# Cosine attention followed by a token-mixing MLP: a hand-written order of instructions changed in ten places

## The chip, the cores and the metric

The kernel runs on one core of one Trainium2 chip. The metric is device time in microseconds (us) of one execution; lower is better. The engines are named as in the profile: PE (TensorE matmul) and PEld (its weight loads), DVE (VectorE), ACT (ScalarE), POOL (GpSimd), and SP (SyncE), which here issues every DMA.

## The reference

Two operations follow each other. With B = 8 batches, 8 heads, S = 576 positions and head size 64, in float32:

```python
r = np.maximum(x, 0.0)                                  # for q and k
phi = np.concatenate([r * cos_w, r * sin_w], axis=-1)   # 64 -> 128 features
kv  = np.einsum('bhsf,bhsd->bhfd', k_p, v)
z   = np.sum(k_p, axis=2)
num = np.einsum('bhsf,bhfd->bhsd', q_p, kv)
den = np.einsum('bhsf,bhf->bhs', q_p, z)[..., None] + 1e-06
x   = num / den                                         # back to (B, S, 512)

wq, wk = x @ w_q, x @ w_k                               # 512 -> 64
W_tok  = scale * np.einsum('bsd,btd->bst', wq, wk)
mixed  = np.einsum('bst,btd->bsd', W_tok, x)
out    = np.maximum(mixed, 0.0) @ w_out                 # 512 x 512
```

The kernel takes the second part as wq @ (wk^T x), so that no 576 x 576 matrix is made.

## The kernel before

The work is cut into 16 **halves** H (half the heads of a batch; H = 2b + h) for the attention, 8 **batches** b for the mixing, and 36 **row tiles** of 128 rows for the product with w_out. Each piece of work is a small function, a *step*. One long string, ORDER, lists the steps; the kernel walks it once and issues each step's instructions on its engine. An engine runs its instructions in the order in which they were issued and waits where an operand or a buffer isn't ready, so ORDER sets the order on each engine. A word such as `QT10:2` or `EP22@A` is a step, its number, after a colon the PSUM bank from which it writes (eight banks, most results take a pair), and after @ the engine (A = ACT, V = DVE, G = POOL). A trailing a or b is one half of a step whose work is split in two.

The steps of a half H:

- LK, LQ, LV: loads of k, q, v (two DMAs each, 288 KB); five buffers of each, used in turn.
- RK, RQ: relu to bf16 (lines 203, 205). CV, VS: v to bf16 (209, 211), then multiplied by the cos and sin table on DVE (line 234); VG does both in one on POOL (line 248).
- QT: q transposed on PE (line 295 "wide", 9 transposes of 128x128; line 301 "narrow", 18 of 64 rows). The tuple QT_WIDE says which halves are wide. QM multiplies that by the table on DVE: two instructions for a wide half (line 316), one for a narrow one (line 320).
- KV: the kv matrix on PE (lines 275, 285); KE takes it out of PSUM (lines 209, 213).
- N(2H), N(2H+1): numerator and denominator on PE (line 340; some have two short matmuls more, line 348, that add epsilon). EP adds epsilon to the denominator (357 on ACT, 359 on DVE), RC and RJ are reciprocals (378, 381), X multiplies (line 393), all into the token matrix x of the batch.

The steps of a batch b: XT or XR transpose x on PE (406, 419), XE takes that out into xT (209, 213); WK and WQ are the products with w_k and w_q on PE (439, 452), KW and QW take them out; KX is wk^T x on PE (466), XK takes it out, XA and XB copy it to the other partitions; MX is the mixing product on PE (489, four a batch: MX(4b) to MX(4b+3)), ME its relu (500 on ACT, 502 on DVE).

WO is a row tile's product with w_out on PE (line 509, four matmuls of 128x512), OE takes it out into one of 16 output buffers (the number behind its colon), ST stores it (line 519, 256 KB). WO needs only mixed batches, so WO steps stand between other steps all the way to the end.

PSUM banks, output buffers and the pairs of buffers of most tiles are written again while the kernel runs; a step that writes one waits for the step that read it last. So the bank number in a word decides for whom the step waits.

Of the kernel before, what the change touches and what calls it, by code (L numbers as in the profile page):

```python
# [37 lines left out]
EP8@V EP9@V RJ4 RQ6a@A XT5:0 X8 XB1@G XE5@A X9 KV7:2 RQ6b@G QM7 VG6b MX6:4 KE7@A XT4:0 ME6@A MX7:2
XE4@V QT6:6 ME7@A N15:4 QM6 RK6a@A MX3:2 N14:0 CV6a@G LV11a EP15@A RK6b@A WK2:6 ME3@A VS6a WQ2:7
KW2@A RC14 KV6:2 RC15 QW2@A X14 CV8a@G KX2:7 KE6@A CW4@G X15 CW2@A N13:2 CW3@A CW5@V N12:0 EP13@V  # L40
XR7:4 XK2@V WO8:6 RC13 XA2@A X13 EP12@A CV8b@G XE7@A WO2:7 RC12 VS8 WO7:2 CV9b@A RQ8a@G LQ13a LQ11b
LQ10a LK11b LK11a LQ11a LV11b X12 OE8:0@A MX8:4 WO6:3 RQ8b@A RK8a@G ME8@V OE7:1@A XR6:0 RQ9a@G WO1:6
CV9a@A XE6@V RQ9b@G OE2:2@A QT8:4 VS9 OE6:3@A RK8b@A QT9:0 RK9a@G OE1:4@A WK3:3 QM9 WO4:2 RK9b@G
KW3@A OE4:5@A ST4 LV12a LK10a LQ10b LV10a LV10b LQ12a KV8:0 QM8 XB2@A KV9:6 KE8@A MX9:4 KE9@A MX11:0
VG11a N16:2 ME9@A ME11@V WQ3:6 RC16 KX3:7 X16 QW3@A MX10:0 XK3@A N17:4 ME10@A N19:2 RK11@V N18:6
EP19@A WO11:0 EP17@V RQ11@A RC17 EP18@V X17 WO5:1 VG11b OE11:6@V ST11 LK12a LK10b LQ13b LV12b LK12b
LQ12b QT11:4 OE5:5@A RC19 RC18 X18 WO9:0 X19 WO10:1 OE9:7@A RQ10@G KV11:2 XA3@A QM11 XR8:6 KE11@A
XR9:4 VG10a LV15a LV13a LQ14b LV14b LQ14a LV13b XE8@A QT10:2 XE9@V WO0:5 QM10 OE10:8@A MX13:0
OE0:6@A MX12:6 N22:2 WO12:4 RQ13a@G ME12@V EP22@A XB3@A ME13@A RC22 VG10b WK4:5 X22 MX14:0 KW4@A
N23:6 ME14@V MX15:2 EP23@A KX4:5 RK10@A WQ4:0 XK4@V RQ13b@G RC23 WO3:1 ME15@A X23 XA4@G XB4@A QW4@A  # L50
RQ12b@G KV10:2 OE3:9@V RQ12a@A QT13:6 OE12:10@A ST12 LK13b LK13a LV14a VG12 MX18:0 WO14:5 QM13
# [3 lines left out]
EP24@V RK13@A RJ12 QT14:0 X24 WO21:2 KW5@A X25 CV14a@G KV13:4 OE21:10@A ST21 LQ15b LQ15a ST3 LK15a
QM14 CV14b@A WQ5:3 KE13@A KX5:2 VS14 XR12:4 XK5@A N27:0 XE12@A N26:6 RK14a@G WO20:2 RC26 EP27@V RC27
XA5@G RK14b@A X27 WO19:4 XB5@G QW5@A VG15b X26 KV14:0 OE19:2@A MX21:6 KE14@A MX23:4 WO18:3 ME21@V
ME23@A OE20:10@V ST20 ST17 ST8 ST9 XR13:4 RQ15a@G MX22:6 RQ15b@V MX20:0 ME22@A WO15:2 VG15a XE13@V
ME20@A N28:6 OE18:9@V OE15:14@A N29:0 EP28@A QT15:4 RK15@A EP29@V RC28 WK6:3 RC29 X29 WO25:2 KW6@A
QM15 OE25:15@A ST25 ST7 ST15 ST18 ST0 ST10 ST16 ST5 ST14 ST6 KV15:0 X28 KX6:3 KE15@A WQ6:2 N31:0  # L60
XR14:6 EP31@V QW6@A N30:4 XE14@V WO23:2 EP30@A XK6@A RJ15 X30 XA6@G WO24:3 OE23:7@A ST23 ST1 XB6@G
X31 WO26:2 OE24:0@A ST24 ST19 XR15:0 MX25:4 MX27:6 XE15@V ME25@A WO22:3 ME27@V WK7:0 OE26:9@V ST26
MX24:6 KW7@A MX26:4 WQ7:1 ME24@A ME26@V KX7:0 OE22:8@V ST22 WO28:2 XK7@A QW7@V XA7@G WO27:3
# [7 lines left out]
def kernel(  # L71
# [240 lines left out]
    def QM(H, ps, eng):  # L312
        if H in QT_WIDE:
            q_t = qt_wide(place["QT", H]).rearrange("p c (r d) -> p r c d", r=2)
            for r in range(2):
                V.tensor_mul(  # L316
                    qm_b[H % NQM][:, :, r, 0:C, :],
                    q_t[:, r].unsqueeze(1).to_broadcast([P, 2, C, H2]), qtab)
# [280 lines left out]
```

## Time and profile before

| what | value |
|---|---|
| time, median of 3 runs | 119.17 us (118.6 to 119.84) |
| the profiled execution: its own time / its span | 118.42 / 116.6 us |
| PE busy | 94.7 us (81% of the span) |
| DVE, ACT, POOL busy | 90.5, 83.1, 64.8 us |
| DMA | 39.38 MB, mean 338 GB/s |
| granted TensorE clock | 1.000 |

The span runs from the first to the last instruction; the execution's own time is 1.8 us longer. In the timelines that follow, each row is a run of equal instructions: start in us from the beginning of the span, time from the first start to the last end, engine, line, operation, output <- inputs, and the count; in brackets the engine's idle time ahead of it and what ended that. Rows of PE overlap a little, since matmuls are pipelined: the next row's start tells where the row's work has left the engine.

### The profile page before, as it was taken

Reading aid. Unit: us, or ns where it says so; the run is one execution under the profiler, and the core shown is the slowest. Engines: PE = TensorE matmul, PEld = TensorE weight load, DVE = VectorE, ACT = ScalarE, POOL = GpSimd, SP = SyncE. Lnnn points to the kernel's source line nnn. Section 1 sums busy time; section 2 is a strip of 40 time slices with the busy share of each in tenths; the row PEclk is TensorE's granted clock in tenths of the full one; section 3 lists DMA queues with packets and bytes.
Section 4 is the critical chain, followed back from the end, with each engine's and each line's share of the span. In section 5 each row is a group of like instructions: output and inputs, shape, how many; then the busy total and the mean of one; then the engine's idle time right before and its main releaser. Section 6 shows DMA issues by size and latency. Waiting matters only on the chain.

```text
span 116.6 us, 4971 instructions
## 1 busy us (share of the span) xinstructions
PE 94.7 (81%) x2104; PEld 65.1 (56%) x2118; DVE 90.5 (78%) x162; ACT 83.1 (71%) x147; POOL 64.8 (56%) x65
## 2 busy tenths in 40 slices
PE   0005967779796797999999899999999999999970
PEld 0004856657576776647775656656775576463420
DVE  2008999799798999889799887898997996795620
ACT  4547558499899987898884878986888774546340
POOL 7600399861634796477298498899659901002000
PEclk9999999999999999999999999999999999999999
DMA  3999999999999999999979999987898467999874
GB/s 90 349 386 399 401 372 346 388 389 396 386 392 384 387 387 387 391 390 384 383 251 302 351 397 371 358 266 258 270 340 293 169 236 271 403 367 400 337 306 173
DMA packets 20662, 39.38 MB, mean 338 GB/s; under 512 B 3232, under 2 KB 3232, under 8 KB 20640
## 3 DMA queue, kind: packets, MB, share of 16 engines
q1 hardware_dynamic: 20640, 39.07, 92.4%
q8 instruction: 16, 0.26, 0.9%
q14 instruction: 6, 0.05, 0.1%
HBM read 29.62 MB, written 9.44 MB: 335 GB/s over the span
## 4 chain that ended last, share of the span: by engine, by line
PE 48%; DMA 26%; DVE 14%; SPq 4%; issue 3%; ACT 1%; DVEq 0%; ACTq 0%
PE ps L509 24%; DMA qraw<-in_q_dram 16%; DMA vraw<-in_v_dram 5%; DMA kraw<-in_k_dram 5%; PE ps L340 5%; DVE qm L316 5%; SPq L145 4%; PE ps L285 3%; PE ps L489 3%; PE ps L419 3%; PE ps L439 3%; DVE xT L213 3%; PE ps L466 3%; PE ps L452 2%; DVE x L393 2%
## 5 line engine op out<-in xcount | busy, mean ns | idle before, releaser
L248 POOL TENSOR_TENSOR v<-vraw,vtab 128x1152 bf16<-128x1152 f32 (+1 forms) x12 | 35.5, 2969 | 6.5 <-DVE qm L316 2.2
L509 PE MATMUL ps<-wow,mix 128*128 128x512 bf16 x130 | 33.3, 380 | 1.2 <-issue 0.3
L393 DVE TENSOR_TENSOR x<-ps,rec 128x640 bf16<-128x640 f32 x32 | 25.4, 818 | 0.7
L209 ACT COPY o<-ps 128x512 f32<-128x512 f32 x25 | 14.5, 592 | 9.2 <-PE ps L509 8.1
L509 PEld LDWEIGHTS <-mix 128*128 128x128 bf16 x144 | 12.5, 98 | 14.4 <-issue 1.7
L295 PE MATMUL ps<-ident,rq 128*128 128x128 bf16 x117 | 9.5, 233 | 12.0 <-ACT rq L203 11.0
L316 DVE TENSOR_TENSOR qm<-ps,qtab 128x1152 bf16<-128x1152 bf16 x26 | 18.3, 749 | 0.8 <-PE ps L295 0.7
L234 DVE TENSOR_TENSOR v<-vb,vtab 128x2304 bf16<-128x2304 bf16 (+1 forms) x11 | 11.8, 1084 | 7.7 <-ACT vb L209 7.3
L500 ACT ACTIVATE mix<-ps 128x576 bf16<-128x576 f32 x23 | 14.5, 651 | 3.5 <-PE ps L489 2.5
L340 PE MATMUL ps<-kvs,qm 64*128 64x65 bf16 x640 | 14.0, 193 | 2.1 <-ACT kvs L209 1.3
L295 PEld LDWEIGHTS <-rq 128*128 128x128 bf16 x117 | 7.6, 104 | 13.6 <-issue 10.5
L340 PEld LDWEIGHTS <-qm 64*128 64x128 bf16 x640 | 12.6, 96 | 4.2 <-issue 2.3
L203 ACT ACTIVATE rk<-kraw 128x1152 bf16<-128x1152 f32 (+1 forms) x14 | 14.0, 996 | 0.7 <-DMA kraw<-in_k_dram 0.7
L205 POOL TENSOR_SCALAR rq<-qraw 128x576 bf16<-128x576 f32 (+1 forms) x13 | 10.1, 776 | 4.4 <-DMA qraw<-in_q_dram 3.5
L211 POOL TENSOR_SCALAR vb<-vraw 128x576 bf16<-128x576 f32 (+1 forms) x7 | 5.7, 810 | 11.9 <-DMA vraw<-in_v_dram 8.8
L211 POOL TENSOR_SCALAR kx<-kx 64x256 bf16<-64x256 bf16 x9 | 4.1, 457 | 12.6 <-ACT kx L209 11.0
L502 DVE TENSOR_SCALAR mix<-ps 128x576 bf16<-128x576 f32 x9 | 6.8, 757 | 4.0 <-PE ps L489 3.8
L285 PE MATMUL ps<-v,rk 64*64 64x130 bf16 x432 | 9.1, 231 | 0.8 <-POOL v L248 0.7
L209 ACT CAST kvs<-ps 128x260 bf16<-128x260 f32 (+1 forms) x15 | 6.5, 436 | 4.6 <-PE ps L285 3.9
L285 PEld LDWEIGHTS <-rk 64*64 64x64 bf16 x432 | 7.5, 114 | 3.9 <-issue 1.2
L203 ACT ACTIVATE rq<-qraw 128x576 bf16<-128x576 f32 (+1 forms) x10 | 8.3, 832 | 1.1 <-DMA qraw<-in_q_dram 1.1
L213 DVE COPY xT<-ps 128x1280 bf16<-128x1280 bf16 (+1 forms) x9 | 7.3, 813 | 2.2 <-PE ps L419 2.0
(65 smaller groups left out, 137.3 us busy)
## 6 DMA issues: line engine op xcount, KB each, us to landing
kraw<-in_k_dram SPq DMA_DIRECT2D x32, 288.0 KB, 5.9
qraw<-in_q_dram SPq DMA_DIRECT2D x32, 288.0 KB, 5.9
vraw<-in_v_dram SPq DMA_DIRECT2D x32, 288.0 KB, 5.8
out_dram<-o SPq DMA_DIRECT2D x36, 256.0 KB, 3.4
wof<-in_moe_w_out_dram SPq DMA_DIRECT2D x4, 256.0 KB, 5.8
wkf<-in_moe_w_k_dram SPq DMA_DIRECT2D x1, 128.0 KB, 5.7
wqf<-in_moe_w_q_dram SPq DMA_DIRECT2D x1, 128.0 KB, 6.2
```

The source lines that it names most:

```text
L203: A.activation(dst, s, AF.Relu)
L209: A.copy(dst, s)
L213: V.tensor_copy(dst, s)
L234: V.tensor_mul(v2_b[H % NV2][:, part, :, :, 0:D], vb_b[H % NPREP][:, part].unsqueeze(3).to_broadcast([P, n, C, 2, D]), vtab.unsqueeze(1).t ...
L248: G.tensor_mul(dst[:, part, :, :, 0:D], s[:, part].unsqueeze(3).to_broadcast([P, n, C, 2, D]), vtab.unsqueeze(1).to_broadcast([P, n, C, 2, ...
L285: nc.tensor.matmul(kv_v[o, r, :], rk_of(H)[a, pr, c, :], v2_b[H % NV2][a, pr, c, :, 0:D + 1], start=(c == 0), stop=(c == C - 1))
L295: nc.tensor.transpose(qt_v[:, c, :], rq_b[H % NPREP][:, c, :, :], ident)
L316: V.tensor_mul(qm_b[H % NQM][:, :, r, 0:C, :], q_t[:, r].unsqueeze(1).to_broadcast([P, 2, C, H2]), qtab)
L340: nc.tensor.matmul(nv[:, pr, u, :], qm_b[H % NQM][a, s, r, 2 * u:2 * u + 2, :], kv_b[H % 2][a, r, pr if H in KV_WIDE else 0, s, 0:D + 1], ...
L393: V.tensor_tensor(x_b[b % NX][:, :, 4 * h:4 * h + 4, :].rearrange("p u (w r) d -> p r w u d", r=2)[:, r], nv[:, :, :, 0:D], rec(g).to_broa ...
L500: A.activation(dst, s, AF.Relu, scale=scale_moe)
L509: nc.tensor.matmul(o, mix_b[bp % 2][:, m, rt * P:(rt + 1) * P], wow[:, m, :], start=(m == 0), stop=(m == NDM - 1))
```

## The change

The string ORDER is changed in these places (in the order of the program), and half 10 leaves QT_WIDE:

1. `N0:6 N1:4 RC2 EP0@V EP1@V X2` becomes `N1:4 RC2 N0:6 EP1@V X2 EP0@V`; a little later `XR0:4 KE3@A CW1@A` becomes `KE3@A CW1@A XR0:4`, which moves nothing on any engine.
2. `VS7` becomes `VS7b VS7a`: one DVE multiplication of 128x2304 becomes two of 128x1152.
3. `WK2` moves from behind MX3, N14 to ahead of them, directly behind N15; its bank is 2 instead of 6. MX3 takes bank 0, N14 bank 6, WQ2 bank 3, KV6 bank 0.
4. `EP12@A` (behind X13) becomes `EP12@V`, directly behind EP13.
5. `MX9:4` moves from behind KV9 to behind N16, so MX11 comes first.
6. `OE11:6@V` becomes `OE11:6@A`; the load LQ12a moves from ahead of KV8 to behind the store ST11.
7. `WO10` moves from ahead of KV11 to behind QT10; QT10 and QM10 are narrow.
8. `N22` moves from behind MX12 to ahead of QM10 and MX13, in bank 6; MX12 takes bank 2, N23 bank 2, MX15 bank 6.
9. `RC23` moves ahead of WQ4 and XK4; `X23` from behind WO3 to behind XK4.
10. `ST16` moves from the late stores (behind ST10) to ahead of the load LQ15b.

```diff
-RC11 X10 CV7a@A CV7b@G X11 MX5:6 MX4:0 KE4@A RQ7b@G RQ7a@A VS7 N8:2 N9:4 ME5@A ME4@A QT7:6 RK7@G
+RC11 X10 CV7a@A CV7b@G X11 MX5:6 MX4:0 KE4@A RQ7b@G RQ7a@A VS7b VS7a N8:2 N9:4 ME5@A ME4@A QT7:6
...
-    QT_WIDE = (0, 1, 2, 3, 4, 5, 6, 7, 8, 9, 10, 11, 14)
+    QT_WIDE = (0, 1, 2, 3, 4, 5, 6, 7, 8, 9, 11, 14)
```

On DVE, at VS7 (v is the product, vb the bf16 copy of v, vtab the table; the rows ahead are X10, X11, those behind EP8, EP9 and RJ4):

```order
 L378 RECIPROCAL rec_91<-rec_91 128x10
 L393 TENSOR_TENSOR x_94<-ps,rec_91 128x2x5x64 x2
-L234 TENSOR_TENSOR v_85<-vb_83,vtab 128x36x64
+L234 TENSOR_TENSOR v_85<-vb_83,vtab 128x18x64 x2
 L359 TENSOR_SCALAR rec_90<-ps 128x10 x2
 L381 RECIPROCAL rec_90<-rec_90 128x20
```

Nothing changes place; the instruction is cut in two, of which the first (VS7b) needs the copy made by POOL and the second (VS7a) the copy made by ACT.

On PE, at WK2 (line 340 is N15 and, between the rows of line 489 and line 348, N14; 489 is MX3, 439 is WK2, 452 is WQ2; rows of LDWEIGHTS and MATMUL alternate, "..." leaves the repeats out):

```order
 L340 LDWEIGHTS qm_87
 L340 MATMUL ps<-kvs_89,qm_87 128x65
+L439 LDWEIGHTS xT_96
+L439 MATMUL ps<-wkw,xT_96 128x64
...
 L489 LDWEIGHTS kx_102
 L489 MATMUL ps<-wq_100,kx_102 128x288
...
 L348 MATMUL ps<-epsr,ones 128x5
-L439 LDWEIGHTS xT_96
-L439 MATMUL ps<-wkw,xT_96 128x64
...
 L452 LDWEIGHTS wqw
```

WK2's 20 matmuls stand between N15 and MX3 now, and WQ2 follows directly on N14.

On DVE, around QM10 (o is OE11's output, the following rows are RC19 and RC18, X18 and X19, QM11, XE9, QM10, ME12, RC22 and X22, ME14):

```order
-L213 COPY o_112<-ps 128x512
 L378 RECIPROCAL rec_91<-rec_91 128x10 x2
 L393 TENSOR_TENSOR x_94<-ps,rec_91 128x2x5x64 x2
 L316 TENSOR_TENSOR qm_87<-ps,qtab 128x2x576 x2
 L213 COPY xT_96<-ps 128x2x2x5x64
-L316 TENSOR_TENSOR qm_86<-ps,qtab 128x2x576 x2
+L320 TENSOR_TENSOR qm_86<-ps,qtab 128x4x576
 L502 TENSOR_SCALAR mix_105<-ps 128x576
```

OE11 leaves DVE for ACT, where it stands between RQ11 and OE5, and QM10 is one instruction. On PE the rows of the same stretch were WO9, WO10, KV11, XR8, XR9, QT10, WO0, MX13, MX12, N22, WO12, and are now WO9, KV11, XR8, XR9, QT10, WO10, WO0, N22, MX13, MX12, WO12.

More of the change, by code (lines that the diff above doesn't have):

```diff
@@ L29 @@
 RK1b@V RQ0@V KV1:2 QM1 QT0:4 KE1@A CV0@G LV5b LV5a RK0@A LK5b LK5a LQ5a LQ5b LQ4b LQ4a N2:2 VS0 N3:0
-VG3 QM0 KV0:6 KE0@A RC3 EP2@A X3 RQ3@A N0:6 N1:4 RC2 EP0@V EP1@V X2 RK3@A QT3:0 RC0 XT1:2 X0 XE1@A
-RC1 X1 VG2b KV3:6 QM3 XR0:4 KE3@A CW1@A N6:0 XE0@V EP6@A N7:6 CW0@G EP7@A WK0:4 VG2a RQ2@A WQ0:5
+VG3 QM0 KV0:6 KE0@A RC3 EP2@A X3 RQ3@A N1:4 RC2 N0:6 EP1@V X2 EP0@V RK3@A QT3:0 RC0 XT1:2 X0 XE1@A
+RC1 X1 VG2b KV3:6 QM3 KE3@A CW1@A XR0:4 N6:0 XE0@V EP6@A N7:6 CW0@G EP7@A WK0:4 VG2a RQ2@A WQ0:5
 KW0@V RC6 KX0:4 X6 RK2@A LK7a LV4a LV4b LK4a LK4b LV7a LV7b LQ7b LQ7a LQ6a LK7b LV6b LQ6b LW2 LK6b
@@ L36 @@
 WQ1:3 RC10 KW1@A VS4 RK4@A LK9a LK8b LK9b KX1:2 MX2:6 N11:4 XK1@V QW1@A ME2@A EP11@V KV4:2 XA1@A
-RC11 X10 CV7a@A CV7b@G X11 MX5:6 MX4:0 KE4@A RQ7b@G RQ7a@A VS7 N8:2 N9:4 ME5@A ME4@A QT7:6 RK7@G
[L38 to L51, printed above, removed]
+RC11 X10 CV7a@A CV7b@G X11 MX5:6 MX4:0 KE4@A RQ7b@G RQ7a@A VS7b VS7a N8:2 N9:4 ME5@A ME4@A QT7:6
@@ new lines @@
+RK7@G EP8@V EP9@V RJ4 RQ6a@A XT5:0 X8 XB1@G XE5@A X9 KV7:2 RQ6b@G QM7 VG6b MX6:4 KE7@A XT4:0 ME6@A
+MX7:2 XE4@V QT6:6 ME7@A N15:4 WK2:2 QM6 RK6a@A MX3:0 N14:6 CV6a@G LV11a EP15@A RK6b@A ME3@A VS6a
+WQ2:3 KW2@A RC14 KV6:0 RC15 QW2@A X14 CV8a@G KX2:7 KE6@A CW4@G X15 CW2@A N13:2 CW3@A CW5@V N12:0
+EP13@V XR7:4 EP12@V XK2@V WO8:6 RC13 XA2@A X13 CV8b@G XE7@A WO2:7 RC12 VS8 WO7:2 CV9b@A RQ8a@G LQ13a
+LQ11b LQ10a LK11b LK11a LQ11a LV11b X12 OE8:0@A MX8:4 WO6:3 RQ8b@A RK8a@G ME8@V OE7:1@A XR6:0 RQ9a@G
@@ new lines @@
+WO1:6 CV9a@A XE6@V RQ9b@G OE2:2@A QT8:4 VS9 OE6:3@A RK8b@A QT9:0 RK9a@G OE1:4@A WK3:3 QM9 WO4:2
+RK9b@G KW3@A OE4:5@A ST4 LV12a LK10a LQ10b LV10a LV10b KV8:0 QM8 XB2@A KV9:6 KE8@A KE9@A MX11:0
+VG11a N16:2 MX9:4 ME9@A ME11@V WQ3:6 RC16 KX3:7 X16 QW3@A MX10:0 XK3@A N17:4 ME10@A N19:2 RK11@V
+N18:6 EP19@A WO11:0 EP17@V RQ11@A RC17 EP18@V X17 WO5:1 VG11b OE11:6@A ST11 LQ12a LK12a LK10b LQ13b
+LV12b LK12b LQ12b QT11:4 OE5:5@A RC19 RC18 X18 WO9:0 X19 OE9:7@A RQ10@G KV11:2 XA3@A QM11 XR8:6
+KE11@A XR9:4 VG10a LV15a LV13a LQ14b LV14b LQ14a LV13b XE8@A QT10:2 WO10:1 XE9@V WO0:5 N22:6 QM10
@@ L52 @@
+OE10:8@A MX13:0 OE0:6@A MX12:2 WO12:4 RQ13a@G ME12@V EP22@A XB3@A ME13@A RC22 VG10b WK4:5 X22 MX14:0
+KW4@A N23:2 ME14@V MX15:6 EP23@A KX4:5 RK10@A RC23 WQ4:0 XK4@V X23 RQ13b@G WO3:1 ME15@A XA4@G XB4@A
+QW4@A RQ12b@G KV10:2 OE3:9@V RQ12a@A QT13:6 OE12:10@A ST12 LK13b LK13a LV14a VG12 MX18:0 WO14:5 QM13
 KE10@A ME18@A XR11:2 OE14:11@A MX16:0 N21:6 XE11@V ME16@A N20:4 EP21@A EP20@V RK12@A QT12:0 RJ10 X21
@@ L54 @@
 ME19@A WO17:3 OE16:12@A KE12@V XE10@V MX17:0 OE17:13@A N25:6 ME17@V N24:4 RQ14a@A WK5:3 EP25@V
[L55 to L63, printed above, removed]
+EP24@V RK13@A RJ12 QT14:0 X24 WO21:2 KW5@A X25 CV14a@G KV13:4 OE21:10@A ST21 ST16 LQ15b LQ15a ST3
+LK15a QM14 CV14b@A WQ5:3 KE13@A KX5:2 VS14 XR12:4 XK5@A N27:0 XE12@A N26:6 RK14a@G WO20:2 RC26
+EP27@V RC27 XA5@G RK14b@A X27 WO19:4 XB5@G QW5@A VG15b X26 KV14:0 OE19:2@A MX21:6 KE14@A MX23:4
+WO18:3 ME21@V ME23@A OE20:10@V ST20 ST17 ST8 ST9 XR13:4 RQ15a@G MX22:6 RQ15b@V MX20:0 ME22@A WO15:2
+VG15a XE13@V ME20@A N28:6 OE18:9@V OE15:14@A N29:0 EP28@A QT15:4 RK15@A EP29@V RC28 WK6:3 RC29 X29
+WO25:2 KW6@A QM15 OE25:15@A ST25 ST7 ST15 ST18 ST0 ST10 ST5 ST14 ST6 KV15:0 X28 KX6:3 KE15@A WQ6:2
+N31:0 XR14:6 EP31@V QW6@A N30:4 XE14@V WO23:2 EP30@A XK6@A RJ15 X30 XA6@G WO24:3 OE23:7@A ST23 ST1
+XB6@G X31 WO26:2 OE24:0@A ST24 ST19 XR15:0 MX25:4 MX27:6 XE15@V ME25@A WO22:3 ME27@V WK7:0 OE26:9@V
+ST26 MX24:6 KW7@A MX26:4 WQ7:1 ME24@A ME26@V KX7:0 OE22:8@V ST22 WO28:2 XK7@A QW7@V XA7@G WO27:3
 OE28:11@A ST28 XB7@G MX31:0 MX28:4 MX30:6 ME31@V ME28@A WO29:2 ME30@A OE27:7@V ST27 MX29:4 OE29:4@V
```

## Prediction

> **What bounds the kernel now.** I read the DMA first, in the table of busy times by stretches; its share of time and GB/s stand last in the row.
>
> ```profile
> 40.00:50.00 10.00, 8.97 (x226) 6.93 (x228) 9.33 (x19) 8.46 (x16) 6.69 (x8) 1.00 1.05 387
> ```
>
> At 40 to 50 us the DMA engines are full (1.05, 387 GB/s): the loads set the pace, and no order of the other engines makes them faster. PE is busy for 9 of 10 us and fills up from there. So I look at what PE waits for from 44.6 us to the end, and then at the last long piece of the chain of waits:
>
> ```profile
> PE ps L439 <- DVE qm L316: 0.7, 1, 0.7
> ...
> PE ps L509 <- DVE xT L213: 0.3, 1, 0.3
> ...
> 107.72 5.30 PE ps L509 x24
> ```
>
> In nearly 70 us PE has two waits with a named cause, 1.0 us together, and the run ends on PE: 24 matmuls of WO, with only a copy and a store behind them. So the change can gain by the 0.7 us at WK2, the 0.3 us at WO0, PE work that becomes less, and whatever makes DVE's qm at 44.6 us earlier. That ceiling is about 1.5 us, an estimate with 0.4 us for the last.
>
> **VS7 in two.** The chain into the 0.7 us wait is DVE's:
>
> ```profile
> 35.67 1.50 DVE L393 TENSOR_TENSOR x<-ps,rec 128x640 bf16<-128x640 f32 x2
> 37.59 1.36 DVE L234 TENSOR_TENSOR v<-vb,vtab 128x2304 bf16<-128x2304 bf16 x1 [0.42 <-ACT kvs L209]
> 42.41 0.76 DVE L213 COPY xT<-ps 128x1152 bf16<-128x1152 bf16 x1
> 43.19 1.42 DVE L316 TENSOR_TENSOR qm<-ps,qtab 128x1152 bf16<-128x1152 bf16 x2
> 44.52 0.75 DVE L234 TENSOR_TENSOR v<-vb,vtab 128x1152 bf16<-128x1152 bf16 x1
> 45.19 0.21 DVE L378 RECIPROCAL rec<-ps 128x10 f32<-128x10 f32 x1
> 35.51 0.67 POOL L211 TENSOR_SCALAR vb<-vraw 128x576 bf16<-128x576 f32 x1 [1.88 <-DVE rec L359]
> 37.62 0.80 PE L340 MATMUL ps<-kvs,qm 64*128 64x65 bf16 x40 [0.76 <-ACT kvs L209]
> ```
>
> DVE is free at 37.17 (35.67 + 1.50), but VS7 starts 0.42 later, when an ACT instruction ends, and is done at 38.95. VS7b needs only POOL's half, ready at 36.18, so it can start at 37.17; VS7a follows after that ACT instruction. A half takes 0.75 us, and 0.67 from start to start (44.52 to 45.19): VS7a starts at 37.84 and is done at 38.59, 0.36 us earlier; N9, which the next step reads, ends at 38.42. If the idle time stays, it is done at 37.59 + 0.67 + 0.75 = 39.01, 0.06 later. So the bounds are 0.06 lost and 0.36 gained; I take 0.35 gained, since the row names an ACT instruction and the order takes ACT off the first half. It passes on whole: from here to qm's end at 44.61 DVE's largest idle time is 0.07 us (at 42.41), and PE's steps in between wait for DVE. **Term A: -0.35 us.**
>
> One rule makes this edit dangerous. While a DVE multiplication with two SBUF inputs runs, POOL's relu is held:
>
> ```profile
> 53.82 1.48 POOL L205 TENSOR_SCALAR rk<-kraw 128x576 bf16<-128x576 f32 x1 [0.72 <-DMA kraw<-in_k_dram]
> 38.52 1.44 POOL L205 TENSOR_SCALAR rk<-kraw 128x1152 bf16<-128x1152 f32 x1 [1.58 <-DMA kraw<-in_k_dram]
> ```
>
> A POOL instruction of that size takes 0.67 us (the row at 35.51), this relu 1.48; VS9, 1.35 us on DVE, runs beside it. So a POOL relu that gets in between VS7b and VS7a would hold VS7a. The Trainium skill, "SBUF — State Buffer", "Who interferes with whom", says that the one issued first keeps the shared ports for its whole instruction and the other blocks fully; the trace agrees with 1.48 against 0.67 us. By that rule the cut opens a place where RK7 can go first; this is the slower rival below.
>
> **WK2 ahead.** The same wait on PE:
>
> ```profile
> 43.08 0.49 PE L340 MATMUL ps<-kvs,qm 64*128 64x65 bf16 x20
> 43.40 0.28 PE L489 MATMUL ps<-wq,kx 64*128 64x288 bf16 x2
> 43.52 0.47 PE L340 MATMUL ps<-kvs,qm 64*128 64x65 bf16 x20
> 44.66 0.74 PE L439 MATMUL ps<-wkw,xT 128*128 128x64 bf16 x20 [0.66 <-DVE qm L316]
> 45.33 0.68 PE L452 MATMUL ps<-xT,wqw 128*64 128x288 bf16 x8
> ```
>
> WK2 waited for QM6 (qm, end 44.61) only because of bank 6. In bank 2 it can start at 43.40, xT being ready at 43.17 (42.41 + 0.76); it takes 0.67 (44.66 to 45.33), MX3 0.12 more: 44.19. Now N14 has bank 6 and waits for QM6 to 44.66, takes 0.47 to its end, its short epsilon matmuls beside it: WQ2 starts at 45.13 instead of 45.33. **Term B: -0.20 us**; it can't pass -0.35, as most of N14 always follows QM6, and it is above zero only if WK2 doesn't start before QM6 ends. Behind the new wait of N14 stand WQ2 and KV6; RC14, which reads N14, starts at 45.19 anyway (the row above). With A, all of this is 0.35 us earlier. Do the loads permit this lead of 0.55? The tightest product of a load that I find up to 57 us is CV8b, which VS8 reads:
>
> ```profile
> 47.84 0.68 POOL L211 TENSOR_SCALAR vb<-vraw 128x576 bf16<-128x576 f32 x1 [1.22 <-DMA vraw<-in_v_dram]
> 49.38 1.29 DVE L234 TENSOR_TENSOR v<-vb,vtab 128x2304 bf16<-128x2304 bf16 x1
> ```
>
> It is done at 48.52, 0.86 us ahead of its reader: enough. EP12 on DVE has to wait for N12 there, a part of the idle time that DVE has ahead of XE6 anyway, and leaves ACT.
>
> **Half 10, WO10, N22 and OE11 together.** PE, ACT and DVE, in before's times:
>
> ```profile
> 62.78 1.89 PE L509 MATMUL ps<-wow,mix 128*128 128x512 bf16 x8
> 64.60 0.72 PE L285 MATMUL ps<-v,rk 64*64 64x130 bf16 x36
> 65.25 0.76 PE L419 MATMUL ps<-ident,x 64*128 64x64 bf16 x40
> 66.93 1.02 PE L509 MATMUL ps<-wow,mix 128*128 128x512 bf16 x3 [0.31 <-DVE xT L213]
> 67.89 0.42 PE L489 MATMUL ps<-wq,kx 64*128 64x288 bf16 x4
> 68.26 0.49 PE L340 MATMUL ps<-kvs,qm 64*128 64x65 bf16 x20
> 68.68 1.04 PE L509 MATMUL ps<-wow,mix 128*128 128x512 bf16 x4
> 93.01 0.42 PE L301 MATMUL ps<-ident,rq 64*128 64x64 bf16 x18
> 62.52 0.59 ACT L209 COPY o<-ps 128x512 f32<-128x512 f32 x1 [0.83 <-PE ps L509]
> 61.69 0.69 DVE L213 COPY o<-ps 128x512 f32<-128x512 f32 x1
> 62.61 1.56 DVE L393 TENSOR_TENSOR x<-ps,rec 128x640 bf16<-128x640 f32 x2
> 64.08 1.41 DVE L316 TENSOR_TENSOR qm<-ps,qtab 128x1152 bf16<-128x1152 bf16 x2
> 66.06 0.82 DVE L213 COPY xT<-ps 128x1280 bf16<-128x1280 bf16 x1 [0.56 <-PE ps L419]
> ```
>
> Before, WO0 waits at 66.93 for XE9 (xT, end 66.88), whose bank it writes. With WO10 taken out, KV11 follows on WO9 at 63.75 (a lone WO, 0.97). It needs X19 out of its bank: that ended at 64.17, but OE11 (61.69; 0.60 of its 0.69 until the next one starts) is off DVE, so 63.57. KV11 takes 0.65, XR8 0.38 (half of 0.76): 64.78. XR9 needs QM11 out of its bank, end 65.49 - 0.60 = 64.89; so it starts at 64.93 and ends at 65.31. QT10 narrow takes 0.42 (the row at 93.01): 65.73. WO10 and WO0 take 1.82 (62.78 to 64.60): 67.55; XE9, 0.82 us behind XR9, has ended at about 66.2. N22 0.42, MX13 and MX12 0.37: WO12 starts at 68.34, not 68.68. **Term C: -0.34 us**, bounds 0 (DVE no earlier, then KV11 and XR9 wait what WO0 waited) and -0.5 (no wait at XR9 either). OE11 on ACT, 0.59 us, fits in the 0.83 us that ACT is idle ahead of OE5 (62.52). QM10 is one instruction about as long as its two were.
>
> **The rest I cost at nothing.** N1 ahead of N0 lies where the loads set the pace; MX9 behind N16 trades places with MX11 within 0.3 us, since QM8 holds one and KE8 the other. RC23 fits in DVE's idle time ahead of XK4. ST11 and ST16 are old results; each puts 256 KB, about 0.65 us at 390 GB/s, ahead of loads. The load with least room is LQ15a:
>
> ```profile
> 90.50 0.67 POOL L205 TENSOR_SCALAR rq<-qraw 128x576 bf16<-128x576 f32 x1
> 91.13 2.38 POOL L248 TENSOR_TENSOR v<-vraw,vtab 128x1152 bf16<-128x1152 f32 x1
> 94.92 0.72 PE L285 MATMUL ps<-v,rk 64*64 64x130 bf16 x36
> ```
>
> RQ15a starts without a wait, VG15a behind it ends at 93.51, KV15 reads it at 94.92: 1.41 us of room for 0.65. In exchange, one store fewer stands in the last 20 us.
>
> **Sum.** -0.35 - 0.20 - 0.34 = -0.89 us, carried by a full PE to the last store. For the profiled execution, 118.42 becomes 117.5; it was faster than all three runs shown, whose median is 119.17, so the forecast for a median is **118.3 us**.
>
> **Rivals.**
> (1) *VS7's idle time stays* (+0.06 for -0.35): -0.48, **118.7**. For it: the row's ACT instruction is KE4, which VS7 doesn't read. Against: it started just as that ended.
> (2) *The lead is given back at X23.* MX15 now writes N22's bank and waits for X22, KV10 writes N23's and waits for X23:
>
> ```profile
> 71.74 0.43 DVE L213 CAST kx<-ps 128x256 bf16<-128x256 f32 x1 [0.34 <-PE ps L466]
> 72.32 0.82 DVE L393 TENSOR_TENSOR x<-ps,rec 128x640 bf16<-128x640 f32 x1
> 73.03 0.72 PE L285 MATMUL ps<-v,rk 64*64 64x130 bf16 x36
> ```
>
> With a lead of 0.89 KV10 wants to start at 72.14; X23, directly behind XK4, ends at 70.85 + 0.43 + 0.82 = 72.10. That is just enough, and it is the point from which this decides. If X23 kept 73.14, KV10 would start 0.15 us later than before, **119.3**; halfway, **118.8**.
> (3) *Slower: RK7 goes between VS7b and VS7a*, and holds DVE for a relu of 128x1152: 1.0 us, the 1.44 of its row less the 0.43 for which VS7 was still running. A becomes +0.65, the sum +0.11, **119.3**. It decides by when RK7's load lands: RK7 started at 38.52, and the gap between the halves is at 37.84, or at 38.26 if the idle time stays; a load 0.3 to 0.7 us earlier would do it.
> (4) *Nothing of it reaches the end*, as the last stores are held by DMA: **119.2**. Against it: the chain's last 5 us are PE's, and there is one store less.
>
> **Chances.** Forecast 0.45, (1) 0.20, (2) 0.18, (3) 0.07, (4) 0.05, and 0.05 for what I don't see. Runs of before differ by 1.2 us, so a median is good to about 0.6, and under 1% (1.19 us) this kernel can hardly be told from no change. Faster by over 1% (below 117.98) needs the forecast with all terms at their better ends: 0.30. Slower by over 1% (above 120.36) needs rival 3 or an unseen cause and a bad spread: 0.08. Within 1%: 0.62. Range: 117.2 (better ends, -0.35 - 0.35 - 0.5 = -1.2, which is 117.97, and some spread of the runs) to 119.6 (rivals 2 and 3 and a little spread).
>
> **What would show it.** A: VS7b starts at about 37.2 with no idle time ahead. B: the list of PE's waits has no 0.7 at L439; N14 waits instead, and WQ2 starts by 44.8. C: no idle time at WO0, QT10 a row of 18, WO12 (four of L509 behind L489) at 67.8. The end: PE's last matmuls end at about 112.1. Waits of PE at MX15 or KV10 on DVE's x (L393) would show rival (2); a wait of POOL or PE on LQ15a would show that a store ahead of loads costs more than its 0.65 us.

## The result, and the profile after

| | kernel before | changed kernel |
|---|---|---|
| time, median of 22 runs each | 119.16 us (118.24 to 120.64) | 118.33 us (117.43 to 120.31) |
| the profiled execution: its own time / its span | 118.42 / 116.6 us | 118.43 / 116.7 us |
| PE, DVE, ACT, POOL busy | 94.7, 90.5, 83.1, 64.8 us | 94.6, 90.7, 83.3, 63.0 us |

The ratio is 0.9914, with a 95% interval of 0.9891 to 0.9937; runs that were disturbed on the chip are left out of the ratios, here and below. The forecast was 118.3 us. But the two profiled executions are equally long, so the profile has to explain two things: where the gain comes from, and why this execution does not show it at its end. They are not quite like for like: that of before is shorter than all but one of the 22 runs of its kernel, that of the changed kernel lies near its median.

The table by stretches, what PE waits for from 44.6 us on, and the end of the chain of waits, of the changed kernel, and at last a line of the kernel before:

```profile
40.00:50.00 10.00, 9.77 (x232) 6.97 (x231) 9.42 (x19) 8.61 (x16) 6.55 (x8) 1.00 1.05 389
...
PE ps L285 <- issue: 0.7, 2, 0.5
PE ps L509 <- issue: 0.5, 3, 0.2
PE ps L285 <- DVE qm L316: 0.2, 1, 0.2
...
107.71 5.30 PE ps L509 x24
...
PE ps L509 <- issue: 0.3, 2, 0.2
```

PE is busy for 9.77 us of 40 to 50 (8.97 before), the waits of 0.7 at WK2 and 0.3 at WO0 are gone, and yet the last 24 matmuls begin at 107.71 (107.72 before). In their place stand waits named "issue": PE stood still, and no semaphore shows why. The small ones at L509 are not new: two of them stand in the kernel before as well, and each, 0.16 us, is at a row of WO that lacks the record of one matmul (x3 or x7), so it need not be a stop. New are the two at L285. The timelines at the three places of the prediction, DVE first, then PE:

```profile
37.23 1.42 DVE L234 TENSOR_TENSOR v<-vb,vtab 128x1152 bf16<-128x1152 bf16 x2
42.93 1.42 DVE L316 TENSOR_TENSOR qm<-ps,qtab 128x1152 bf16<-128x1152 bf16 x2
...
43.24 0.76 PE L439 MATMUL ps<-wkw,xT 128*128 128x64 bf16 x20
44.41 0.49 PE L340 MATMUL ps<-kvs,qm 64*128 64x65 bf16 x20 [0.18 <-DVE qm L316]
44.83 0.68 PE L452 MATMUL ps<-xT,wqw 128*64 128x288 bf16 x8
...
62.05 0.67 PE L295 MATMUL ps<-ident,rq 128*128 128x128 bf16 x9
64.81 0.47 PE L419 MATMUL ps<-ident,x 64*128 64x64 bf16 x20 [0.18 <-DVE qm L316]
65.10 0.44 PE L301 MATMUL ps<-ident,rq 64*128 64x64 bf16 x18
67.31 0.48 PE L340 MATMUL ps<-kvs,qm 64*128 64x65 bf16 x20
67.97 1.04 PE L509 MATMUL ps<-wow,mix 128*128 128x512 bf16 x4
72.33 0.72 PE L285 MATMUL ps<-v,rk 64*64 64x130 bf16 x36
```

VS7 ends at 38.65 (38.95 before), WQ2 starts 0.50 us earlier than before (44.83 against 45.33), QT11 0.23 (62.05 against 62.28), WO12 0.71 (67.97 against 68.68) and KV10 0.70 (72.33 against 73.03). So the lead (by how much the same work starts earlier than in the kernel before) was there, fell to 0.23 between 45 and 62 us, and rose again. Where it fell, and where all of it went at last, PE's rows show, of the changed kernel and then of the kernel before:

```profile
55.74 1.06 PE L285 MATMUL ps<-v,rk 64*64 64x130 bf16 x59 [0.19 <-DVE qm L316]
57.00 0.39 PE L285 MATMUL ps<-v,rk 64*64 64x130 bf16 x13 [0.19 <-issue]
88.09 0.54 PE L285 MATMUL ps<-v,rk 64*64 64x130 bf16 x22
89.09 0.42 PE L285 MATMUL ps<-v,rk 64*64 64x130 bf16 x14 [0.47 <-issue]
89.44 0.42 PE L489 MATMUL ps<-wq,kx 64*128 64x288 bf16 x4
...
56.16 1.24 PE L285 MATMUL ps<-v,rk 64*64 64x130 bf16 x72
62.28 0.67 PE L295 MATMUL ps<-ident,rq 128*128 128x128 bf16 x9
88.80 0.72 PE L285 MATMUL ps<-v,rk 64*64 64x130 bf16 x36
89.45 0.42 PE L489 MATMUL ps<-wq,kx 64*128 64x288 bf16 x4
```

KV14 starts 0.71 us earlier than before, takes 1.35 us instead of 0.65, and what follows is 0.01 us ahead. It stops in the middle, after 22 of its 36 matmuls, all of which read the same rk and v. KV9 stops after 23 of its 36: the row of 59 is KV8 with these 23, and 13 are left; before, KV8 and KV9 are one row of 72. Counted in the order of the program, these two places lie 1536 instructions of PE apart, six times 256: 767 matmuls, as many weight loads, and two instructions that only wait for a semaphore. And the page has a line for DMA packets that carry instructions; in a stretch of 1 us ahead of KV14's stop there is one:

```profile
q8 instruction: 16, 0.26, 0.9%
...
q8 instruction: 1, 0.02, 5.5%
```

The first line is of the whole page: 16 packets of 16 KB, and PE's rows in the trace come from about 4270 instructions, 16.7 times 256 (2127 weight loads, as many matmuls, and a few that only wait). The second is of the stretch 86.6 to 87.6 us; 83.6 to 86.6 and 87.6 to 89.2 have no such line.

**Theory.** PE's instructions come in blocks of 256, each by one 16 KB packet that is asked for when PE enters the block ahead, and that goes through the DMA engines among the loads and stores. If it comes late, PE stops at the block's first instruction, and a lead over the kernel before is lost there. **Rivals:** the stop belongs to KV14's data (its load LK14a landed late, and RK14a on POOL with it), to the store ST16 now ahead of loads, or it is chance; and one of the three terms does all the work.

The Trainium skill, "Runtime: NRT & Kernel Launch", "Instruction fetch mechanics", says that an engine's instructions are refilled in 16 KiB blocks of 256, that the next block is fetched while the present one runs, and that the cost of crossing into it is mostly hidden. The trace agrees with the size and the count; hidden it is not here, with 0.47 us at KV14.

### The profile page after: what moved, and what is told of

Read it like the earlier page. It is cut to its first block, busy times and chain, and to the rows that moved or that the text cites. A ratio compares the mean times of both kernels' runs of the same rounds, so it can differ in the third digit from the quotient of the medians.

```text
span 116.7 us, 4987 instructions
## 1 busy us (share of the span) xinstructions
PE 94.6 (81%) x2113; PEld 64.2 (55%) x2127; DVE 90.7 (78%) x162; ACT 83.3 (71%) x147; POOL 63.0 (54%) x65
## 4 chain that ended last, share of the span: by engine, by line
PE 46%; DMA 26%; DVE 14%; issue 4%; ACT 4%; SPq 3%; DVEq 0%; ACTq 0%
PE ps L509 22%; DMA qraw<-in_q_dram 11%; DMA kraw<-in_k_dram 10%; DMA vraw<-in_v_dram 5%; PE ps L285 4%; PE ps L340 4%; DVE qm L316 4%; DVE x L393 3%; SPq L145 3%; PE ps L489 3%; PE ps L419 3%; PE ps L439 2%; PE ps L466 2%; DVE xT L213 2%; PE ps L452 2%
## 5 line engine op out<-in xcount | busy, mean ns | idle before, releaser
L509 PE MATMUL ps<-wow,mix 128*128 128x512 bf16 x130 | 33.1, 380 | 1.0 <-issue 0.5
L209 ACT COPY o<-ps 128x512 f32<-128x512 f32 x26 | 15.1, 589 | 8.8 <-PE ps L509 7.2
L509 PEld LDWEIGHTS <-mix 128*128 128x128 bf16 x144 | 12.4, 98 | 14.3 <-issue 1.8
L295 PE MATMUL ps<-ident,rq 128*128 128x128 bf16 x108 | 8.8, 235 | 12.3 <-ACT rq L203 11.6
L234 DVE TENSOR_TENSOR v<-vb,vtab 128x1152 bf16<-128x1152 bf16 (+1 forms) x12 | 12.0, 1022 | 7.2 <-ACT vb L209 7.2
L316 DVE TENSOR_TENSOR qm<-ps,qtab 128x1152 bf16<-128x1152 bf16 x24 | 16.9, 749 | 0.8 <-ACT kvs L209 0.4
L295 PEld LDWEIGHTS <-rq 128*128 128x128 bf16 x108 | 7.1, 105 | 13.8 <-issue 10.2
L285 PE MATMUL ps<-v,rk 64*64 64x130 bf16 x432 | 9.5, 227 | 1.5 <-POOL v L248 0.7
L285 PEld LDWEIGHTS <-rk 64*64 64x64 bf16 x432 | 7.4, 110 | 5.1 <-issue 1.9
```

The costliest lines, as they stand in the source:

```text
L209: A.copy(dst, s)
L234: V.tensor_mul(v2_b[H % NV2][:, part, :, :, 0:D], vb_b[H % NPREP][:, part].unsqueeze(3).to_broadcast([P, n, C, 2, D]), vtab.unsqueeze(1).t ...
L285: nc.tensor.matmul(kv_v[o, r, :], rk_of(H)[a, pr, c, :], v2_b[H % NV2][a, pr, c, :, 0:D + 1], start=(c == 0), stop=(c == C - 1))
L295: nc.tensor.transpose(qt_v[:, c, :], rq_b[H % NPREP][:, c, :, :], ident)
L316: V.tensor_mul(qm_b[H % NQM][:, :, r, 0:C, :], q_t[:, r].unsqueeze(1).to_broadcast([P, 2, C, H2]), qtab)
L509: nc.tensor.matmul(o, mix_b[bp % 2][:, m, rt * P:(rt + 1) * P], wow[:, m, :], start=(m == 0), stop=(m == NDM - 1))
```

## The experiments

Each kernel was timed in rounds beside the kernel before. In all of them but after_again ORDER takes two lines less, so that line numbers are two lower than above (L283 for L285). dummy36 has 4 runs, c_only and st16_back 6, the others 12. The ratios:

| kernel | median, us | ratio to before, 95% interval |
|---|---|---|
| a_only | 118.65 | 0.9955 (0.9921 to 0.9990) |
| b_only | 119.39 | 1.0023 (0.9985 to 1.0062) |
| c_only | 117.90 | 0.9872 (0.9836 to 0.9908) |
| a_c | 118.00 | 0.9914 (0.9878 to 0.9951) |
| no_b | 118.81 | 0.9950 (0.9901 to 0.9999) |
| st16_back | 118.15 | 0.9893 (0.9841 to 0.9944) |
| after_again | 118.89 | 0.9926 (0.9875 to 0.9976) |
| dummy128 | 118.71 | 0.9934 (0.9887 to 0.9981) |
| dummy108 | 119.52 | 0.9978 (0.9927 to 1.0028) |
| dummy36 | 121.65 | 1.0189 (1.0093 to 1.0286) |
| early | 118.76 | 0.9940 (0.9899 to 0.9981) |
| c_early | 119.05 | 0.9998 (0.9958 to 1.0039) |

### The three terms one by one

**a_only**

```diff
-VS7
+VS7b VS7a
```

> The kernel before with VS7 in two operations and nothing else. Theory (the sum of the prediction): VS7b starts at about 37.2 us with no idle time ahead of it, everything from EP8 to QM6 is 0.25 to 0.35 us earlier, and so is the end: 0.35 us less than the kernel before (ratio 0.997). Rival one: the lead of 0.35 us is there up to 55 us but not at the end, because PE waits later for something that no semaphore shows: ratio 1.000. Rival two: VS7's idle time stays, ratio 1.000, and no lead anywhere.

DVE's rows at VS7, XE4 and QM6:

```profile
37.04 1.42 DVE L232 TENSOR_TENSOR v<-vb,vtab 128x1152 bf16<-128x1152 bf16 x2
42.23 0.76 DVE L211 COPY xT<-ps 128x1152 bf16<-128x1152 bf16 x1 [0.32 <-PE ps L404]
43.01 1.42 DVE L314 TENSOR_TENSOR qm<-ps,qtab 128x1152 bf16<-128x1152 bf16 x2
```

No idle time ahead of VS7b, and VS7 ends at 38.46, 0.49 us earlier than before. QM6 starts only 0.18 us earlier (43.19 before), less than expected: XE4 ahead of it waits 0.32 us for PE's transposes, so here the lead did not pass on whole. Ratio 0.9955: the first term alone is worth something at the end, 0.1 to 0.9 us by its interval, which holds the 0.35 of the sum. Rival two falls.

**b_only**

```diff
-N15:4 QM6 RK6a@A MX3:2 N14:0 ... WK2:6 ME3@A VS6a WQ2:7 KW2@A RC14 KV6:2
+N15:4 WK2:2 QM6 RK6a@A MX3:0 N14:6 ... ME3@A VS6a WQ2:3 KW2@A RC14 KV6:0
```

> The kernel before with WK2 ahead of MX3 and N14 and the five bank numbers that go with it, nothing else. Theory: the wait of 0.7 us at L439 goes, WQ2 starts at 45.1 instead of 45.3 us, and the time falls by 0.20 us (ratio 0.998). Rival one: the lead is there at 45 us and gone at the end (ratio 1.000). Rival two: PE's wait at N14 for qm is as long as that at WK2 was, no lead at WQ2 either.

PE's rows at N15, N14 and WQ2, and at KV14:

```profile
43.67 0.49 PE L338 MATMUL ps<-kvs,qm 64*128 64x65 bf16 x20
45.25 0.49 PE L338 MATMUL ps<-kvs,qm 64*128 64x65 bf16 x20 [0.18 <-DVE qm L314]
45.68 0.56 PE L450 MATMUL ps<-xT,wqw 128*64 128x288 bf16 x6
...
89.70 0.66 PE L283 MATMUL ps<-v,rk 64*64 64x130 bf16 x32
90.93 0.25 PE L283 MATMUL ps<-v,rk 64*64 64x130 bf16 x4 [0.57 <-issue]
```

The wait of 0.7 is 0.18 here. This execution is late from earlier on (N15 starts at 43.67, at 43.08 before), but from N15 to WQ2 it needs 2.01 us instead of 2.25: the term is there, 0.24 us. At the end no gain is to be seen (1.0023), and there are stops. That at KV14 tells most: it comes after the 32nd matmul, not the 22nd. Half 10 is wide here, 9 transposes instead of 18, so 18 instructions fewer stand ahead of KV14, and a border of 256 lies 9 to 10 matmuls later in it. Data would not know that.

**c_only**

```diff
-OE11:6@V ... WO9:0 X19 WO10:1 ... QT10:2 XE9@V WO0:5 QM10 ... MX12:6 N22:2 ... N23:6 ... MX15:2
+OE11:6@A ... WO9:0 X19 ... QT10:2 WO10:1 XE9@V WO0:5 N22:6 QM10 ... MX12:2 ... N23:2 ... MX15:6
-KX4:5 RK10@A WQ4:0 XK4@V RQ13b@G RC23 WO3:1 ME15@A X23
+KX4:5 RK10@A RC23 WQ4:0 XK4@V X23 RQ13b@G WO3:1 ME15@A
-    QT_WIDE = (0, 1, 2, 3, 4, 5, 6, 7, 8, 9, 10, 11, 14)
+    QT_WIDE = (0, 1, 2, 3, 4, 5, 6, 7, 8, 9, 11, 14)
```

> The kernel before with the third term alone: WO10 behind QT10, half 10 narrow, N22 ahead with its banks, OE11 on ACT, RC23 and X23 earlier; loads and stores in their places of before. Theory: no idle time at WO0, the group of WO12 starts 0.34 us earlier than in the kernel before (68.3 instead of 68.7 us; 0.5 at most), and the time falls by 0.34 us (ratio 0.997). Rival: the two executions profiled so far end at the same time although the changed one is 0.71 us ahead from 71 to 88 us, since PE stands still for 0.47 us in the middle of KV14, at an instruction that waits for no semaphore; if that belongs to the lead, it shows here as well, as a short stop of PE named issue between 84 and 92 us, and the ratio is 1.000.

PE's only wait with a name from 44.6 us on, its rows at QT11, WO12 and KV14:

```profile
PE ps L437 <- DVE qm L314: 0.7, 1, 0.7
...
62.13 0.67 PE L293 MATMUL ps<-ident,rq 128*128 128x128 bf16 x9
68.03 1.04 PE L507 MATMUL ps<-wow,mix 128*128 128x512 bf16 x4
88.34 0.72 PE L283 MATMUL ps<-v,rk 64*64 64x130 bf16 x36
```

Between QT11 and WO12 this execution gains 0.50 us on the one of before (its lead goes from 0.15 to 0.65 us), and KV14 has no stop. WO12 starts earlier than expected (68.03 for 68.3). The lead is 0.46 at KV14 and the span 0.4 us shorter (116.2 against 116.6). The ratio says 1.3%, 1.5 us, far more than the 0.34 expected, though from only six runs; the trace accounts for a third of that.

**st16_back** (ST16 from ahead of LQ15b back to behind ST10)

> The changed kernel with ST16 among the late stores again. Theory of the prediction: a store ahead of loads costs nothing here and one store fewer stands at the end, which costs nothing either: the same time as the changed kernel, ratio 0.991 against the kernel before. Rival: the 256 KB of ST16 stand ahead of something that PE needs at KV14 (a load, or PE's own instructions, whose 16 KB packets use the same DMA engines); then the stop of PE at KV14 is shorter than 0.47 us and the time 0.2 to 0.5 us below the changed kernel's (ratio 0.987 to 0.990).

```profile
88.48 0.54 PE L283 MATMUL ps<-v,rk 64*64 64x130 bf16 x22
89.73 0.42 PE L283 MATMUL ps<-v,rk 64*64 64x130 bf16 x14 [0.72 <-issue]
```

The stop is at the same matmul and longer than in the changed kernel (0.72 against 0.47 us), so ST16 is not its cause. The time, 0.9893, can't be told from the changed kernel's, nor from the 0.987 to 0.990 of the rival.

**no_b** (the changed kernel with WK2, MX3, N14, WQ2 and KV6 as before)

> The changed kernel with WK2 and the five banks as before, so that its second term is taken out. Theory of the sum: 0.20 us slower than the changed kernel, ratio 0.993 against the kernel before. Rival, from the four kernels profiled with it alone or left out: where WK2 is ahead, PE's 16 KB blocks of instructions come later after PE has entered the block ahead of them (3.0 to 3.7 us at 45 to 57 us and at 84 us, against 1.1 to 3.0 where it isn't) and PE stops at their first instruction; then this kernel has no stop of PE named issue at KV9 (57 us) and KV14 (88 us), and is faster than the changed kernel by the 0.5 to 0.9 us of those stops, ratio 0.983 to 0.987.

0.9950 is near the sum's 0.993, and its interval leaves out the rival's 0.983 to 0.987. That the second term is not what makes the stops, a_c shows directly: it has stops without WK2's move. Whether the term is worth its 0.2 us can't be told. The one execution that was profiled ran at a granted clock of 0.592 (0.971 or more in all others), so its rows aren't read.

**a_c** (c_only with VS7 in two)

> The kernel before with the first and the third term (VS7 in two, as in a_only, and all of c_only), everything else as before. If the terms add up, ratio 0.983 (0.9955 times 0.987). If a lead at 84 us is worth only what the next block of instructions permits, the first term brings nothing beyond the third: 0.987 to 0.990, with a stop named issue at KV14 in the profile. If the kernel without the second term (no_b, 0.995) shows what the two are worth, 0.993 to 0.997; then c_only's 0.987 was the good end of its spread.

```profile
PE ps L283 <- issue: 0.7, 1, 0.7
...
PE ps L293 <- issue: 0.3, 1, 0.3
...
88.85 0.88 PE L283 MATMUL ps<-v,rk 64*64 64x130 bf16 x36
```

The terms don't add up: 0.9914, not 0.983. Stops stand at KV9 (0.7 us), QT11 (0.3) and, small, at KV14, which takes 0.81 us from its start to MX21's (89.66) instead of 0.65. None of the three ranges expected holds the ratio; 0.990 is nearest. Without WK2's move, and without all that was costed at nothing, the kernel is as fast as the changed one.

### Moving the borders alone

Small matmuls on a constant tile at the start, where PE has nothing to do for 10 us (its first matmul starts at 9.90), change no other instruction; they only move the borders of PE's blocks. Their results are never read.

```diff
-LQ2a LK2a LW0 LV2a LQ2b LK2b TB TI
+LQ2a LK2a LW0 LV2a LQ2b LK2b TB WU146:6 TI
-            nc.tensor.matmul(bank(ps)[0:cols, 0:WARM_COLS], wc[0:rows, WARM_COLS:WARM_COLS + cols],
-                             wc[0:rows, 0:WARM_COLS], start=True, stop=True)
+            m = 64 if n > 1 else WARM_COLS
+            nc.tensor.matmul(bank(ps)[0:cols, 0:m], wc[0:rows, WARM_COLS:WARM_COLS + cols],
+                             wc[0:rows, 0:m], start=True, stop=True)
```

**dummy36**

> The changed kernel with 36 small matmuls more (128x128 by 64 columns, on a constant tile, into bank 6, result never read) at the start, where PE has nothing to do for 12 us. They move every border of 256 instructions of PE's program to 72 instructions earlier in the work. Theory (PE stops where a block of 256 instructions comes late): the stops in KV9 after its 23rd matmul and in KV14 after its 22nd are no longer there; stops named issue come at other instructions, 72 earlier, where the rows of the changed kernel show no idle time (N26 behind XR12 at about 86 us, MX8 and WO6 at 50 us). Because the blocks now hold other work, the time of a block from border to border changes; by the fetch delays of the two profiled executions the stops add up to 1 to 3 us more, 119.5 to 121.5 us. Rival one (the stops belong to KV9's and KV14's data, or to their place in the work): they stay where they are, ratio 0.991. Rival two (chance): no stop anywhere, ratio 0.985.

Rows of PE at its four longest stops:

```profile
49.31 0.47 PE L417 MATMUL ps<-ident,x 64*128 64x64 bf16 x20 [1.53 <-DVE rec L376]
...
62.41 0.59 PE L338 MATMUL ps<-kvs,qm 64*128 64x65 bf16 x27 [0.65 <-issue]
...
79.97 1.90 PE L507 MATMUL ps<-wow,mix 128*128 128x512 bf16 x8 [1.09 <-DVE rec L379]
...
89.06 0.72 PE L338 MATMUL ps<-kvs,qm 64*128 64x65 bf16 x36
90.23 0.24 PE L338 MATMUL ps<-kvs,qm 64*128 64x65 bf16 x4 [0.45 <-issue]
```

The stop of KV14 has moved to N26, after 36 of the 40 matmuls of N27 and N26: 4 of those, 2 of epsilon, 8 of WO20 and WO19 and 22 of KV14 are 36 matmuls, exactly the number added. The time is 1.0189, 2.6% above dummy128 (below), which ran beside it, through instructions that run while PE is idle. A stop can also hide behind a named releaser, as in the row at 79.97: WO16 reads nothing of that reciprocal, and its first instruction lies at a border. The longest, 1.53 us at XR7, is another: its x was done at 46.99, and its first instruction lies at a border too. That one had been expected a little later, at MX8 and WO6.

**dummy128** (WU514: 128 added, 256 instructions)

> The control for the kernel with 36: 128 small matmuls more at the start, 256 instructions with their weight loads, so that every border of a block falls on the same instruction of the work as in the changed kernel. Theory (borders of blocks): the same time as the changed kernel, ratio 0.991, and where PE stops, it stops after the 23rd matmul of KV9 and the 22nd of KV14. Rival (the added matmuls cost something themselves, by their number): more than the kernel with 36.

```profile
88.06 0.54 PE L283 MATMUL ps<-v,rk 64*64 64x130 bf16 x22
89.57 0.42 PE L283 MATMUL ps<-v,rk 64*64 64x130 bf16 x14 [0.98 <-issue]
```

A whole block more: the stop is back after the 22nd matmul of KV14, and the time is the changed kernel's (0.9934). Nothing shows that the added matmuls themselves cost anything. KV9 has no stop in this execution.

**dummy108** (WU434)

> The changed kernel with 108 small matmuls more at the start, which put the borders 40 instructions later in the work than they are. By the delays of the fetches and PE's own rows no block is then shorter than its fetch takes, the stops of PE named issue at KV9 and KV14 go and hardly any comes instead (0.2 us in all): 0.5 us less than the changed kernel, ratio 0.987. Rival one (borders of blocks don't matter): ratio 0.991. Rival two (the fetch delays vary so much from one execution to the next that no place of the borders is better): 0.991, with stops at other instructions than before.

A miss. The profiled execution has no stop at KV9 or KV14, as expected, but the time is 0.9978 (0.9927 to 1.0028), not 0.987: no gain over the changed kernel, perhaps a loss. Rival two is nearest, that one execution's delays don't predict the next one's, but with one profile it is not shown.

### What the packet waits for

**after_again** (the changed kernel, no edit)

> The changed kernel itself, on the same chip and beside the same runs as the next two, for a second profile of it. Theory (PE stops where its next block of 256 instructions comes late): ratio 0.991; a stop named issue, of 0.2 to 1 us, in KV14 after its 22nd matmul, maybe one in KV9 after its 23rd, and no other; each begins less than 1.6 us after the end of the 16 KB packet. Rival (the stop of the first profile was chance): no stop at these two places.

```profile
56.73 0.39 PE L285 MATMUL ps<-v,rk 64*64 64x130 bf16 x13 [0.15 <-issue]
...
PE ps L509 <- ACT wk L209: 1.0, 1, 1.0
PE ps L285 <- issue: 0.2, 1, 0.2
```

KV9 stops at the same matmul (13 left); KV14 loses only 0.16 us. "And no other" was wrong: the largest stop, 1.0 us, is at WO25, at the next border but put down to ACT. So the place of a stop is fixed, and its length differs from one execution to the next.

**early**

```diff
-OE12:10@A ST12 LK13b LK13a LV14a VG12
+OE12:10@A ST12 LK13b LK13a LV14a LK14b LK14a ST2 VG12
-OE13:10@A ST13 LK15b LK14b LK14a LV15b ST2 KV12:6
+OE13:10@A ST13 LK15b LV15b KV12:6
-ST21 ST16 LQ15b LQ15a ... ST0 ST10 ST5
+ST21 LQ15b LQ15a ... ST0 ST10 ST16 ST5
```

> The changed kernel with the loads LK14b and LK14a and the store ST2 directly behind LV14a, into the stretch of 80 to 82 us in which the DMA engines are partly idle, and ST16 among the late stores again. At 84 us, when PE enters the block ahead of KV14's border, fewer transfers are then in the queues. Theory (the packet waits behind data on the DMA engines): its delay falls from 3.0 us to about 1 us, as it has at 79 us in every profile so far (0.4 to 1.0), RK14a on POOL no longer waits for its load, the stop in KV14 goes, and the time falls by 0.5 to 0.9 us against the changed kernel: ratio 0.984 to 0.987. Rival one (the delay doesn't depend on the data in the queues): the stop stays, ratio 0.991. Rival two: the loads come earlier but hold up LV14a's successors or ST13, so that OE21 or VG13 on POOL wait: slower, 0.995.

```profile
83.17 0.48 PE L283 MATMUL ps<-v,rk 64*64 64x130 bf16 x18
84.87 0.48 PE L283 MATMUL ps<-v,rk 64*64 64x130 bf16 x18 [1.22 <-issue]
...
89.55 0.72 PE L283 MATMUL ps<-v,rk 64*64 64x130 bf16 x36
```

The gain did not come (0.9940), the mechanism did: KV14's stop is gone, its packet starting 1.1 us after PE goes on at 84.87, and one of 1.22 us has appeared in KV13, after 18 of its matmuls. From there to KV14's 22nd matmul are 18 of KV13, 8 of WQ5, 10 of KX5, 20 of XR12, 42 of N27 and N26, 8 of WO and 22: 128 matmuls, one block. The packet for the block that begins there starts 0.5 to 1.0 us after PE enters the block ahead, in all nine profiles with this border in KV13 and the transfers unmoved; here, with three transfers moved into that stretch, 4.39 us (3.00 in c_early). Transfers in the queues delay the instructions; moving them moved the stop.

**c_early** (the same moves in c_only, where ST16 had stayed)

> The kernel before with the third term alone (as in c_only, 0.987) and the same transfers moved as in the kernel early. If the stops of PE are what eats the first two terms in the changed kernel, this has them no less than early and lacks 0.3 to 0.5 us of lead: ratio 0.987, slower than early. Rival: the first two terms bring nothing that reaches the end, and the third with the moved transfers is as fast as early or faster (0.984 to 0.987).

ACT's and PE's rows around 85 us:

```profile
84.67 0.58 ACT L207 COPY o<-ps 128x512 f32<-128x512 f32 x1 [1.41 <-DMA out_dram<-o]
...
85.31 0.74 PE L464 MATMUL ps<-x,wk 128*64 128x256 bf16 x10 [0.42 <-ACT o L207]
```

Both expectations missed: all of c_only's gain is gone (0.9998). ST13 lands at 84.57, behind the moved loads, OE21 on ACT waits 1.41 us for its output buffer, and KX5 on PE waits for ACT: the second rival of early, in this kernel.

### Delay and stop at KV14

The records of the 16 KB packets in the trace give their starts; PE's rows give the time from KV14's first matmul to MX21's first. All read profiles with the border inside KV14 and no stop in KV13 (KV13 of c_early takes 0.09 us more than elsewhere):

| kernel | packet starts after PE enters the block ahead, us | KV14 takes, us |
|---|---|---|
| c_early | 1.66 | 0.65 |
| before | 2.07 | 0.65 |
| a_only | 2.25 | 0.65 |
| c_only | 2.27 | 0.66 |
| after_again | 2.62 | 0.81 |
| a_c | 2.67 | 0.81 |
| changed kernel | 3.01 | 1.35 |
| b_only | 3.25 | 1.41 |
| st16_back | 3.40 | 1.61 |
| dummy128 | 3.54 | 1.86 |

Up to 2.3 us the delay is hidden; beyond, KV14 grows nearly as the delay does. PE goes on 1.2 to 1.6 us after the end of the packet in every stop.

## Why the prediction was right or wrong

- *Total.* Right: 118.33 for 118.3 us, ratio 0.9914 for 0.993. That it agrees so closely is in part luck: by their ratios the terms alone came to -0.5, +0.3 and -1.5 us, not -0.35, -0.20 and -0.34, and these add up to -1.8 (with wide intervals), while all together gave -0.8 (medians) to -1.0 (ratio). The five shortest runs of the changed kernel (117.43 to 117.64) lie 0.8 to 1.1 us below the five shortest of before (118.24 to 118.70), which is the sum of 0.89 without loss. That these are runs with hardly a stop is argued only, as none of them was profiled.
- *Term A, -0.35.* VS7b starts at 37.23 without idle time, VS7 ends 0.30 us and QM6 starts 0.26 earlier: near its better bound. Rivals (1) and (3) did not happen: the halves run back to back, 1.42 us for two, and RK7 on POOL starts as VS7a ends, at 38.65. It takes 1.15 us there, so rival (3)'s price of 1.0 us was a little low.
- *Term B, -0.20.* The mechanism held: N14 waits 0.18 us, WQ2 starts at 44.83 (by 44.8 was said), 0.50 earlier, of which A has 0.26. But b_only and a_c show nothing of the 0.24 at the end, and no_b can't tell.
- *Loads permit the lead.* No load stops PE at 45 to 57 us, yet the lead of 0.50 fell to 0.23, by a wait of 0.2 us for qm at KV8 and the stop in KV9, which no row of a load or a buffer could show.
- *Term C, -0.34, at most -0.5.* From QT11 to WO12 the lead grows by 0.48 us (c_only: 0.50). KV11 to N22 came out as worked out (XR9 waits 0.18 us for 0.15); N22 and the two MX were sized at 0.79 us and took 0.66 (67.31 to 67.97), which is the difference.
- *Rival (2), the lead given back at X23.* It wasn't: KV10 is 0.70 us ahead.
- *Stores and LQ15a at nothing.* st16_back agrees within its interval.
- *"Carried by a full PE to the last store".* This step failed. A full PE needs its instructions too, and two blocks came late; in the profiled execution the 0.71 us were gone at KV14, and the last matmuls ended at 113.0, not 112.1. Narrow half 10 also put 18 instructions more into PE's program and moved all later borders by 9 to 10 matmuls, which the prediction did not look at. It kept 0.05 for what it didn't see, and this was it.

**Open.** Why c_only has 0.9872 and a_c, with the first term besides, 0.9914 (the intervals overlap); and what sets the delay within a full queue, 0.8 to 3.9 us between 44 and 62 us. No kernel run here beats the changed one beyond the intervals.

## What to carry to other kernels

When an engine has many short instructions and the DMA engines are full, look at "issue" waits in the middle of a group: count its instructions, and if the stops are a multiple of 256 apart, as PE's were here, the engine may be waiting for its program; a few idle instructions added at the start then move the stops by as many. If so, a lead won upstream is worth only what the next block permits, instructions added or removed anywhere ahead move all later stops, and a moved transfer can hurt without any reader of its data waiting. A single profile shows where such stops can be; how much they cost takes many runs.
